# New orders, PSUM banks and DMA queues for a cross-attention and maxout-FFN kernel

## The chip, the cores and the metric

The kernel runs on one core of a Trainium2 chip. The metric is the device time of one execution in microseconds (us). A core has a matrix engine (PE, with its weight loads shown as PEld), a vector engine (DVE), a scalar engine (ACT), a third elementwise engine (POOL), and SP, which here only starts DMA transfers. ACT and POOL start DMA transfers too, each in its own queue; POOL's transfers also cast float32 to bfloat16 on the way. Matmul results go to PSUM, from where DVE or ACT must copy them before the bank can be used again.

## The reference

```python
scores = scale * x @ state.T            # x: (8, 8, 512, 64), state: (8, 8, 32, 64), scale 1/8
a = softmax(scores);   xread = a @ state
a2 = softmax(scale * state @ x.T);  sread = a2 @ x
t = concat([xread, sread], axis=2)      # 8 batches of 544 tokens, 8 heads of 64
t = t.transpose(0, 2, 1, 3).reshape(4352, 512)
h = maximum(maximum(t @ w1, t @ w2), t @ w3)     # 512 -> 768
out = h @ w_out                                  # 768 -> 512
```

The softmaxes subtract a row's maximum in the reference; the kernel leaves this out on its normal path and looks at the sums at the end (`look`, `flag`, `vl`), to go through a second, safe path only if they have left a range.

## The kernel before

The work of one batch is a chain. x is loaded with a cast to bfloat16 (`lxg` a half with every second head, `lx` the whole; `lxu` loads without a cast and `cxu` casts). It is turned so that the head dimension lies on the partitions: for batches 0 and 1 by PE (`xt`, line 233) with a copy from PSUM (`xtc`), for the others by a transposing DMA on SP's queue (`xtd`, line 245). Scores (`sc`, line 258) go through exp on ACT (`ex`, line 265); DVE sums and takes the reciprocal (`sum`, lines 272 and 274); the weights are the product of both (`wt`, line 280, on POOL or DVE as the plan says). They are turned by PE (`at`, copy `atc`) or by a transposing DMA on SP (`atd`, line 298). The states' read of x is `sr` (line 323), scaled by DVE (`srs`), turned by DMA on SP (`srt`, line 342) and placed (`ap`, line 347). For `sr` of batches 2 on, POOL makes a padded copy of x (`pad`, line 307).

State and W are multiplied first: G = state times W (`g` for a slice of 128 columns of w1, w2 and w3, `gr` for a run of columns, line 359; copies `gc`, `grc` on ACT, DVE, or half each, "AD"). Layer 1 of a batch is then six blocks `l1 b m` (line 412), each three accumulations of 512 columns in three PSUM banks: aT times G. The first goes through ACT (`m0`, line 427), DVE takes the maximum with the second (`ma`, line 432) and the third (`mb`, line 436). Layer 2 (`l2`, line 443) multiplies with w_out four times per batch, each with a copy to the output tile (`l2c`, line 450) and stores for two at a time (`so`, line 473). The states' tokens of all batches go through the same layers at the end as a batch "s" of 256 tokens (`l1s`, `l2 s`, `l2p s`); the end also splits layer 2 of batch 7 into parts of 128 or 256 columns (`l2p`, line 458, copy `l2pc`, store `sop`). W is loaded on POOL's queue by `lw m0 m1 i`: columns 128 m0 to 128 m1 of matrix i; w_out by `lwo` (line 182), states by `lst` (line 150). `busy n` issues n matmuls of zeros into a bank that nobody reads (line 207).

All of this is ordered by hand. Three texts of operations, FIRST, EACH and LAST, are performed in order; every engine takes its instructions in that order and waits only for data and buffers. A letter at the end of an operation is the engine or queue: D DVE, A ACT, P POOL, S SP.

```python
    perform(FIRST)
    for b in range(2, B - 1):
        perform(EACH, b)
    perform(LAST)
```

FIRST holds batches 0 and 1 and the beginning of 2. In EACH the batch number is added to an operation's first number: with -1 layer 2 of the batch before, with 0 layer 1, with 1 scores and G of the next, with 2 and 3 turning and loading x further ahead; an operation for a batch beyond 7 is left out.

PSUM has eight banks: four single ones (b0 to b3) and two pairs (w0, w1). BANKS and PAIRS give, one digit per tile in the order of the text, which one is taken; a tile waits until the copy of the last tile in its bank is done.

```python
    def bank(shape, dtype, name):
        return pp.tile(shape, dtype, tag="b" + next(homes["b"]), bufs=1, name=name)
```

The first steps on POOL's queue are the three cast loads of x (batch 1's first half, batch 0's second, batch 1's second), then W in pieces of 128 to 512 columns.

Of the kernel before, what the change touches and what calls it, by code (L numbers as in the profile page):

```python
# [45 lines left out]
LAST = """
    srt 7; srt 5; l1 7 0; l2 6 3; l1 7 2; ap 5 A; l2 6 1; srt 6; l1 7 3; m0 7 0; ma 7 0; mb 7 0; ap 6 A;
    ap 7 D; m0 7 2; l2c 6 3 D; l2c 6 1 A; l1 7 4; m0 7 3; l1s 0; m0 7 4; ma 7 2; mb 7 2; ma 7 3; mb 7 3;
    l1 7 1; l2 6 0; m0 s 0; ma 7 4; m0 7 1; l2c 6 0 A; ma s 0; mb 7 4; ma 7 1; mb s 0; mb 7 1; l1 7 5;
    m0 7 5; l1s 2; ma 7 5; mb 7 5; m0 s 2; l2p 7 1 384 512; l1s 1; ma s 2; l2p 7 0 384 512; l2p 7 3 256 512;  # L50
    l2pc 7 1 384 512 A; l2 6 2; m0 s 1; sop 7 1 384 512 S; l2p 7 3 0 256; ma s 1; l2p 7 2 128 384;
    l2pc 7 0 384 512 D; l1s 5; l2pc 7 3 256 512 A; l2c 6 2 A; l2p 7 0 0 128; mb s 2; l1s 3; l1s 4; mb s 1;
    l2pc 7 2 128 384 D; m0 s 5; l2p 7 2 0 128; l2p 7 2 384 512; l2p 7 0 128 256; l2pc 7 3 0 256 A;
    l2p 7 1 0 128; m0 s 3; look; ma s 5; sop 7 3 256 512 S; l2pc 7 0 0 128 D; sop 7 2 128 384 S; m0 s 4;
    sop 7 0 384 512 S; mb s 5; sop 7 0 0 128 A; ma s 3; so 6 2 3 P; so 6 1 2 S; so 6 3 4 S; so 6 0 1 P;
    l2pc 7 2 0 128 A; ma s 4; mb s 3; l2p 7 0 256 384; mb s 4; l2pc 7 0 128 256 D; flag; l2p s 0 0 256;
    l2pc 7 2 384 512 A; sop 7 0 128 256 S; sop 7 2 384 512 S; l2pc 7 1 0 128 A; l2pc 7 0 256 384 D;
    l2pc s 0 0 256 D; sop 7 2 0 128 S; l2p 7 1 128 384; l2 s 1; l2p s 0 256 512; sop 7 1 0 128 A;
    l2pc 7 1 128 384 A; sop 7 3 0 256 S; sop 7 0 256 384 S; sop s 0 0 256 S; vl; l2c s 1 D; sop 7 1 128 384 A;
    sos 1 A; l2pc s 0 256 512 D; sop s 0 256 512 A;  # L60
"""
# [606 lines left out]
```

## Time and profile before

| what | value |
|---|---|
| three timed runs | 155.39, 155.70, 155.71 us; median 155.7 |
| the profiled execution | 155.16 us, of which the profile's span is 153.3 |
| busy: PE, DVE, ACT, POOL | 146.6, 108.8, 88.9, 52.0 us |
| layer 1 (288 matmuls of 512 columns), layer 2 (168) | 66.7 and 40.6 us busy |
| fillers (26) | 8.4 us busy, 1.3 to 13.8 us |
| first layer-1 matmul | 16.69 us |
| one round of EACH | 15.25 us |

A timeline row has the start, the length, the engine, the source line, output and inputs with shapes, the number of instructions merged, and in brackets the idle time before with what ended it. PE's rows overlap by design: matmuls are pipelined, so six of 512 columns start within 1.29 us although each is 0.38 us long. The chain of work is followed back from the last instruction; its rows have start, length and work. In the DMA view a row gives the issuing queue, the number of transfers, the size and the median time from issue to landing.

### The profile page before, as it was taken

The numbers are of one execution on the slowest core, as the hardware profiler recorded it, in microseconds if no ns is written. First come the engines' busy times: TensorE is split into PE (matmuls) and PEld (weight loads), VectorE is DVE, ScalarE is ACT, GpSimd is POOL, SyncE is SP. The second block draws the span as 40 slices with busy tenths as digits, with TensorE's granted clock in tenths as the row PEclk, the third lists the DMA queues.
The fourth block names the chain that finished last, engine by engine and source line by source line (L and its number), as shares of the span: only waits on it lengthen the run. The fifth ranks groups of instructions, "written<-read, shape, count | busy, mean of one in ns | idle before, by whom it ended". The sixth has DMA issues, their size and how long they took to land.

```text
span 153.3 us, 3610 instructions
## 1 busy us (share of the span) xinstructions
PE 146.6 (96%) x1429; PEld 73.8 (48%) x1429; DVE 108.8 (71%) x191; ACT 88.9 (58%) x148; POOL 52.0 (34%) x69
## 2 busy tenths in 40 slices
PE   6989999999999999999999999999999999999970
PEld 2566433453454444444444444444344445679940
DVE  3568788799967696778677867786778757645540
ACT  0676887865576577647764776477647644324300
POOL 6999509411229105610571064106410100002000
PEclk9999999999999999999999999999999999999998
DMA  4999999999969997998499930823070300005563
GB/s 117 236 193 203 194 190 194 162 185 195 197 179 166 258 213 220 140 186 166 147 132 194 176 136 3 176 45 137 4 214 17 137 2 4 0 17 193 188 189 114
DMA packets 39477, 22.30 MB, mean 145 GB/s; under 512 B 23584, under 2 KB 37408, under 8 KB 39456
## 3 DMA queue, kind: packets, MB, share of 16 engines
q0 software_dynamic: 14944, 10.75, 40.9%
q1 hardware_dynamic: 22640, 7.21, 27.0%
q10 hardware_dynamic: 1872, 4.06, 7.7%
q8 instruction: 12, 0.20, 0.6%
q14 instruction: 9, 0.07, 0.2%
HBM read 15.20 MB, written 8.91 MB: 157 GB/s over the span
## 4 chain that ended last, share of the span: by engine, by line
PE 88%; DMA 4%; issue 1%; DVE 1%; POOL 1%; ACT 1%; POOLq 0%
PE pw L412 45%; PE po L443 25%; PE pg L359 6%; DMA x<-in_x_dram 4%; PE po L458 4%; PE psr L323 2%; PE ps L258 2%; PE idle L207 1%; POOL x L166 1%; PE pat L291 1%; PE pgh L359 1%; PE pt L218 1%; ACT t L427 0%; DVE xT L240 0%; DVE osb L450 0%
## 5 line engine op out<-in xcount | busy, mean ns | idle before, releaser
L412 PE MATMUL pw<-aT,G 128*128 128x512 bf16 x288 | 66.7, 379 | 0.0
L432 DVE TENSOR_TENSOR t<-t,pw 128x512 bf16<-128x512 bf16 (+1 forms) x54 | 35.1, 650 | 14.7 <-ACT t L427 11.9
L427 ACT CAST t<-pw 128x512 bf16<-128x512 f32 (+1 forms) x54 | 30.8, 569 | 21.9 <-PE pw L412 19.9
L412 PEld LDWEIGHTS <-G 128*128 128x128 bf16 x288 | 27.1, 98 | 33.3 <-issue 1.8
L443 PE MATMUL po<-wout,ht 128*128 128x512 bf16 x168 | 40.6, 379 | 0.1
L436 DVE TENSOR_TENSOR ht<-t,pw 128x512 bf16<-128x512 bf16 x48 | 32.9, 687 | 4.4
L473 POOL DMA_DIRECT2D out_dram<-osb x8 | 4.8, 600 | 66.5 <-ACT osb L450 43.9
L443 PEld LDWEIGHTS <-ht 128*128 128x128 bf16 x168 | 15.3, 97 | 19.6 <-issue 2.7
L450 ACT COPY osb<-po 128x512 f32<-128x512 f32 x24 | 13.6, 590 | 10.9 <-PE po L443 10.9
L399 ACT CAST G<-pg 128x1024 bf16<-128x1024 f32 x18 | 17.7, 1019 | 3.1 <-PE pg L359 3.1
L280 POOL TENSOR_TENSOR a<-e,rden 128x1024 bf16<-128x1024 bf16 (+1 forms) x9 | 14.6, 1640 | 12.9 <-DVE rden L274 6.5
L272 DVE TENSOR_REDUCE seen<-e 128x32 f32<-128x1024 bf16 (+1 forms) x10 | 9.9, 993 | 6.8 <-ACT e L265 6.8
L307 POOL COPY xp<-x 128x1024 bf16<-128x1024 bf16 x12 | 12.3, 1062 | 5.1 <-DMA x<-in_x_dram 5.1
L359 PE MATMUL pg<-w,bd 64*32 64x512 bf16 (+1 forms) x288 | 11.8, 364 | 0.0
L265 ACT ACTIVATE e<-ps 128x1024 bf16<-128x1024 f32 (+1 forms) x10 | 8.5, 854 | 4.1 <-PE ps L258 2.9
L377 ACT CAST G<-pg 128x768 bf16<-128x768 f32 x11 | 8.9, 808 | 2.8 <-PE pg L359 2.8
L207 PE MATMUL idle<-zero 128*128 128x512 bf16 x26 | 8.4, 470 | 1.3 <-DVE zero L185 1.3
L412 PE MATMUL pw<-atp,w 128*128 128x256 bf16 x72 | 8.7, 273 | 0.0
L177 POOL DMA_DIRECT2D w<-in_moe_w_dram x10 | 7.6, 776 | 0.0
L412 PEld LDWEIGHTS <-w 128*128 128x128 bf16 x72 | 7.0, 98 | 1.2
L359 PEld LDWEIGHTS <-bd 64*32 64x32 bf16 x336 | 3.5, 89 | 8.0 <-issue 7.2
L399 DVE CAST G<-pg 128x1024 bf16<-128x1024 f32 x6 | 7.3, 1209 | 0.0
(66 smaller groups left out, 106.5 us busy)
## 6 DMA issues: line engine op xcount, KB each, us to landing
out_dram<-osb ACTq DMA_DIRECT2D x6, 512.0 KB, 4.4
out_dram<-osb POOLq DMA_DIRECT2D x6, 512.0 KB, 3.1
x<-in_x_dram POOLq DMA_DIRECT2D x4, 512.0 KB, 8.3
x<-in_x_dram POOLq DMA_DIRECT2D x7, 256.0 KB, 6.3
w<-in_moe_w_dram POOLq DMA_DIRECT2D x3, 256.0 KB, 8.2
wout<-in_moe_w_out_dram POOLq DMA_DIRECT2D x1, 768.0 KB, 10.0
w<-in_moe_w_dram POOLq DMA_DIRECT2D x5, 128.0 KB, 8.2
osb<-in_x_dram SPq DMA_DIRECT2D x1, 512.0 KB, 4.1
```

The lines of the kernel that those rows point to most:

```text
L207: nc.tensor.matmul(p, zero[:, 0:128], zero, start=True, stop=True)
L272: nc.vector.reduce_sum(out=den, in_=parity(e[b], g), axis=AX.X)
L280: times[c](out=parity(a[b], g).rearrange("p j g s n -> p j (g s) n"), in0=parity(e[b], g).rearrange("p j g s n -> p j (g s) n"), in1=rdens ...
L307: nc.gpsimd.tensor_copy(out=xp[b][:, :, :, g * (D + 1):g * (D + 1) + D], in_=v[:, g])
L359: nc.tensor.matmul(p(s, g), bd(b, 2 * s + g)[64 * g:64 * g + 64, g, :], f(w_sb[64 * g:64 * g + 64, s]), start=True, stop=True, tile_positi ...
L399: copier[c[g]](out=v[:, g:h], in_=p[:, g:h, 0:c1 - c0])
L412: nc.tensor.matmul(pw[i][:, 0:n], lhs(i, k), rhs(k), start=(k == 0), stop=(k == nk - 1))
L427: nc.scalar.copy(out=t0s[b, m][:, 0:n], in_=open_ps["l", b, m][0][:, 0:n])
L432: nc.vector.tensor_max(t1s[b, m][:, 0:n], t0s.pop((b, m))[:, 0:n], open_ps["l", b, m][1][:, 0:n])
L436: nc.vector.tensor_max(ht[b][:, m, :], t1s.pop((b, m))[:, 0:n], open_ps.pop(("l", b, m))[2][:, 0:n])
L443: nc.tensor.matmul(p, ht[b][:, m, j * 128:(j + 1) * 128], wout_sb[:, m, :], start=(m == 0), stop=(m == NM - 1))
L450: copier[c[i]](out=o[:, j, i * w:i * w + w], in_=p[:, i * w:i * w + w])
```

## The change

All plans are written anew; the functions that perform them are the same. In FIRST the fillers are spread in ones and twos, the ACT table is loaded by an early `warm`, W comes in other pieces (columns 0 to 256 of w1 and w3 and 0 to 128 of w2 first; the last pieces are three of 384 columns), `lwo` and half of batch 3's x are issued before `pad 2` and so ahead of batch 2's turning, and some copies change engine (`wt 1 1` to POOL, `wt 2` to DVE, `gc 0 0` to `gc 0 2` to DVE). In EACH, layer 2 of two rows comes before the G runs and scores behind the first block of layer 1; the load of x moves from the round's start to its end, behind a store; the store of rows 0 and 1 moves from ACT's queue to SP's, ahead of `xtd`; `xtd` and `srt` both stand ahead of `atd`. LAST ends on other parts of layer 2, and stores are spread anew over the three queues.

```diff
--- before.py
+++ after.py
@@ -16,57 +16,59 @@
 
 
 FIRST = """
-    zero; busy 10; clr 3; lxu 0 0 S; lxg 1 0; lst 0 A; lxg 0 1; clr 1; busy 1; stc 0 D; clr 0; ident;
-    lxg 1 1; busy 2; lw 0 2 1; stt 0; lst 1 S; cxu 0 0 D; xones 0; xt 0 0; stp 0 A; busy 2; xt 1 0;
-    xtc 0 0 D; sc 0 0; busy 4; warm; xtc 1 0 D; lw 0 1 2; xt 0 1; sc 1 0; lw 0 4 0; xt 1 1; ex 0 0;
-    xtc 0 1 A; sc 0 1; xones 1; sum 0 0; stc 1 P; ex 1 0; lw 1 3 2; xtc 1 1 D; lw 3 5 2; ex 0 1; lw 2 3 1;
-    sum 1 0; sc 1 1; stt 1; busy 6; lw 3 6 1; lxg 2 1; wt 0 0 P; ex 1 1; at 0 0; sum 0 1; sr 0; atc 0 0 A;
-    clr 2; busy 1; wt 1 0 P; stp 1 A; wt 0 1 P; at 1 0; sum 1 1; at 0 1; wt 1 1 D; g 0 0; lxg 2 0; sr 1;
-    atc 0 1 A; srs 1; at 1 1; g 1 0; g 1 1; gc 0 0 A; atc 1 0 D; l1 0 0; atc 1 1 A; ones; g 0 1; gc 1 0 A;
-    gc 1 1 D; m0 0 0; gc 0 1 A; xtd 2; l1 1 0; g 0 2; srs 0; m0 1 0; lw 5 6 0; g 1 2; l1 1 1; ma 0 0;
-    lw 5 6 2; lw 4 5 0; l1 0 1; pad 2; mb 0 0; g 1 3; gc 0 2 A; m0 1 1; gc 1 2 A; ma 1 0; lxg 3 1; g 0 3;
-    l1 0 2; m0 0 1; gc 0 3 A; m0 0 2; l1 1 2; g 0 4; mb 1 0; g 0 5; ma 1 1; l1 0 3; gc 1 3 A; lst 2 A; lwo;
-    mb 1 1; l1 1 3; m0 1 2; ma 0 1; g 1 4; gc 0 4 A; g 1 5; m0 0 3; gc 0 5 A; l1 0 5; mb 0 1; ma 0 2;
-    m0 1 3; mb 0 2; gc 1 4 A; m0 0 5; l1 1 4; ma 1 2; mb 1 2; ma 0 3; ma 1 3; l1 0 4; mb 0 3; mb 1 3;
-    ma 0 5; mb 0 5; m0 1 4; m0 0 4; gc 1 5 A; sc 2 -; lxg 3 0; ma 1 4; mb 1 4; gr 2 1024 1280; lst 3 S;
-    gr 2 0 512; ex 2 -; xtd 3; l1 1 5; ma 0 4; gr 2 512 1024; grc 2 1024 1280 D; lx 4; gr 2 1792 2304;
-    mb 0 4; stc 3 P; sum 2 -; grc 2 0 512 A; grc 2 1792 2304 D; stc 2 P; l2 0 2; m0 1 5; l2 0 3;
-    gr 2 1280 1792; l2c 0 2 D; wt 2 - P; stt 2; grc 2 1280 1792 A; l2 0 1; grc 2 512 1024 A; ma 1 5; mb 1 5;
-    l2 0 0; stp 2 D; stt 3; sr 2; stp 3 A; l2c 0 3 D; so 0 2 4 A; l2c 0 1 D; l2c 0 0 A; srs 2; so 0 0 2 P;
-    atd 2;
+    lxg 1 0; lst 0 A; zero; clr 2; lxg 0 1; busy 1; lst 1 A; busy 2; clr 0; busy 1; busy 1; ident;
+    stc 0 D; lxu 0 0 S; busy 1; busy 1; lxg 1 1; xones 0; lw 0 2 0; clr 3; stt 0; warm; ones; busy 1;
+    busy 1; busy 1; stp 0 DA; busy 1; cxu 0 0 D; busy 1; clr 1; busy 1; lw 0 2 2; xt 0 0; xt 1 0;
+    xtc 1 0 A; busy 2; xtc 0 0 D; busy 1; sc 0 0; lw 0 1 1; xt 0 1; sc 1 0; busy 1; xtc 0 1 D; busy 1;
+    ex 0 0; stc 1 P; sum 0 0; busy 1; ex 1 0; xt 1 1; sc 0 1; xones 1; xtc 1 1 D; busy 1; busy 1; stt 1;
+    lw 1 3 1; lw 2 3 2; busy 1; sc 1 1; lw 2 3 0; wt 0 0 P; lw 3 6 2; busy 1; busy 1; busy 1; ex 0 1;
+    sum 0 1; at 0 0; ex 1 1; lw 3 6 1; busy 1; sum 1 0; sum 1 1; stp 1 A; wt 0 1 P; sr 0; g 0 0; g 1 0;
+    gc 0 0 D; atc 0 0 A; wt 1 0 P; sr 1; at 0 1; srs 0; srs 1; g 0 1; gc 1 0 A; atc 0 1 A; g 1 1;
+    wt 1 1 P; l1 0 0; lw 3 6 0; lxg 2 0; gc 0 1 D; m0 0 0; at 1 0; ma 0 0; gc 1 1 A; at 1 1; g 0 2;
+    lxg 2 1; mb 0 0; g 1 2; gc 0 2 D; atc 1 0 A; atc 1 1 A; l1 0 1; l1 0 2; l1 1 0; m0 0 1; ma 0 1;
+    xtd 2; lst 2 S; l1 1 1; g 0 3; m0 0 2; m0 1 0; mb 0 1; ma 0 2; gc 1 2 A; lwo; m0 1 1; mb 0 2;
+    ma 1 0; ma 1 1; mb 1 0; lxg 3 1; g 1 3; l1 1 2; gc 0 3 AD; gc 1 3 A; g 0 5; m0 1 2; g 1 4; pad 2;
+    l1 0 3; gc 0 5 A; l1 1 3; m0 0 3; gc 1 4 A; mb 1 1; ma 1 2; g 0 4; mb 1 2; m0 1 3; ma 0 3; lxg 3 0;
+    g 1 5; gc 0 4 A; l1 0 5; l1 1 4; stc 2 P; m0 0 5; mb 0 3; gc 1 5 A; ma 1 3; mb 1 3; l1 0 4; ma 0 5;
+    m0 1 4; l1 1 5; m0 0 4; gr 2 512 1024; mb 0 5; m0 1 5; xtd 3; gr 2 1024 1280; ma 1 4; mb 1 4;
+    gr 2 1280 1792; ma 0 4; mb 0 4; ma 1 5; grc 2 1280 1792 A; l2 0 1; sc 2 -; lst 3 A; l2 0 0; l2 0 2;
+    grc 2 1024 1280 AD; ex 2 -; grc 2 512 1024 A; mb 1 5; l2c 0 0 A; stt 2; gr 2 1792 2304; sum 2 -;
+    wt 2 - D; l2c 0 1 D; gr 2 0 512; l2c 0 2 A; sr 2; grc 2 1792 2304 D; stc 3 P; l2 0 3; l2c 0 3 D;
+    so 0 2 4 P; stp 2 A; stt 3; grc 2 0 512 AD; lx 4; so 0 0 2 P; stp 3 A; atd 2; srs 2;
 """
 EACH = """
-    gr 1 1792 2304; lx 3; gr 1 0 512; l2 -1 3; sc 1 -; grc 1 0 512 A; pad 1; l2 -1 0; ex 1 -; l1 0 0;
-    l2 -1 1; grc 1 1792 2304 D; gr 1 1280 1792; gr 1 1024 1280; srt -2; xtd 2; sum 1 -; l2c -1 3 A;
-    gr 1 512 1024; sr 1; l2c -1 0 A; m0 0 0; l1 0 1; ma 0 0; l1 0 2; l2c -1 1 A; so -1 0 2 A; mb 0 0;
-    grc 1 1024 1280 DA; l1 0 3; srs 1; m0 0 1; m0 0 2; ma 0 1; m0 0 3; mb 0 1; wt 1 - P; l1 0 5; m0 0 5;
-    l2 -1 2; grc 1 1280 1792 A; grc 1 512 1024 A; ma 0 2; l1 0 4; mb 0 2; ma 0 3; mb 0 3; ma 0 5; m0 0 4;
-    mb 0 5; ma 0 4; mb 0 4; l2c -1 2 A; atd 1; ap -2 A; so -1 2 4 P;
+    pad 1; l2 -1 0; l2 -1 1; gr 1 1792 2304; gr 1 1024 1280; l2c -1 1 D; l2c -1 0 A; grc 1 1792 2304 AD;
+    gr 1 0 512; l1 0 0; sc 1 -; grc 1 1024 1280 A; so -1 0 2 S; l2 -1 3; m0 0 0; xtd 2; l1 0 1; ex 1 -;
+    gr 1 1280 1792; grc 1 0 512 DA; ma 0 0; mb 0 0; sum 1 -; srt -2; gr 1 512 1024; l2c -1 3 A; m0 0 1;
+    sr 1; l1 0 2; grc 1 1280 1792 A; l1 0 3; ma 0 1; m0 0 2; l1 0 5; wt 1 - P; mb 0 1; srs 1; l1 0 4;
+    ma 0 2; mb 0 2; m0 0 3; m0 0 5; m0 0 4; ma 0 3; mb 0 3; grc 1 512 1024 A; l2 -1 2; ma 0 5; atd 1;
+    l2c -1 2 A; so -1 2 4 P; ma 0 4; mb 0 4; lx 3; mb 0 5; ap -2 A;
 """
 LAST = """
-    srt 7; srt 5; l1 7 0; l2 6 3; l1 7 2; ap 5 A; l2 6 1; srt 6; l1 7 3; m0 7 0; ma 7 0; mb 7 0; ap 6 A;
-    ap 7 D; m0 7 2; l2c 6 3 D; l2c 6 1 A; l1 7 4; m0 7 3; l1s 0; m0 7 4; ma 7 2; mb 7 2; ma 7 3; mb 7 3;
...
-    l2pc 7 2 0 128 A; ma s 4; mb s 3; l2p 7 0 256 384; mb s 4; l2pc 7 0 128 256 D; flag; l2p s 0 0 256;
-    l2pc 7 2 384 512 A; sop 7 0 128 256 S; sop 7 2 384 512 S; l2pc 7 1 0 128 A; l2pc 7 0 256 384 D;
-    l2pc s 0 0 256 D; sop 7 2 0 128 S; l2p 7 1 128 384; l2 s 1; l2p s 0 256 512; sop 7 1 0 128 A;
-    l2pc 7 1 128 384 A; sop 7 3 0 256 S; sop 7 0 256 384 S; sop s 0 0 256 S; vl; l2c s 1 D; sop 7 1 128 384 A;
-    sos 1 A; l2pc s 0 256 512 D; sop s 0 256 512 A;
+    l1 7 0; l2 6 1; m0 7 0; ma 7 0; l2c 6 1 A; mb 7 0; l1 7 2; m0 7 2; srt 7; l1 7 3; m0 7 3; ma 7 2;
+    ma 7 3; l2 6 3; srt 5; ap 5 A; ap 7 A; srt 6; mb 7 2; mb 7 3; l1 7 4; ap 6 A; l2c 6 3 A; m0 7 4;
...
+    l2pc 7 2 384 512 D; sop 7 0 0 128 S; l2p 7 0 128 256; l2p s 0 0 256; l2pc 7 3 0 256 D;
+    l2pc 7 2 0 128 A; l2pc 7 2 128 384 D; l2c s 1 D; l2pc 7 3 256 512 A; l2pc 7 1 128 384 A;
+    l2pc 7 0 128 256 A; flag; sop 7 3 0 256 A; sop 7 2 384 512 A; l2pc s 0 0 256 D; sop 7 0 128 256 A;
+    sop 7 2 0 128 S; sop 7 1 128 384 S; l2 6 2; sop s 0 0 256 A; sop 7 2 128 384 S; sop 7 0 384 512 P;
+    l2p s 0 256 512; l2pc s 0 256 512 D; l2c 6 2 A; l2p 7 1 0 128; so 6 2 3 A; l2pc 7 1 0 128 D;
+    sop 7 0 256 384 S; sos 1 S; sop s 0 256 512 A; sop 7 1 384 512 P; sop 7 1 0 128 A;
+    sop 7 3 256 512 P; vl;
 """
 
 BANKS = """
...
 """
 PAIRS = """
-    0101010110 1010100010 1010010100 1010010100 10
+    0101010110 1010001010 0101001010 0101001010 01
 """
```

More of the change, by code (lines that the diff above doesn't have):

```diff
@@ L45 @@
+    ma 0 2; mb 0 2; m0 0 3; m0 0 5; m0 0 4; ma 0 3; mb 0 3; grc 1 512 1024 A; l2 -1 2; ma 0 5; atd 1;
+    l2c -1 2 A; so -1 2 4 P; ma 0 4; mb 0 4; lx 3; mb 0 5; ap -2 A;
 """
 LAST = """
-    srt 7; srt 5; l1 7 0; l2 6 3; l1 7 2; ap 5 A; l2 6 1; srt 6; l1 7 3; m0 7 0; ma 7 0; mb 7 0; ap 6 A;
-    ap 7 D; m0 7 2; l2c 6 3 D; l2c 6 1 A; l1 7 4; m0 7 3; l1s 0; m0 7 4; ma 7 2; mb 7 2; ma 7 3; mb 7 3;
-    l1 7 1; l2 6 0; m0 s 0; ma 7 4; m0 7 1; l2c 6 0 A; ma s 0; mb 7 4; ma 7 1; mb s 0; mb 7 1; l1 7 5;
@@ L50 @@
[L50 to L54, printed above, removed]
@@ L55 @@
-    sop 7 0 384 512 S; mb s 5; sop 7 0 0 128 A; ma s 3; so 6 2 3 P; so 6 1 2 S; so 6 3 4 S; so 6 0 1 P;
-    l2pc 7 2 0 128 A; ma s 4; mb s 3; l2p 7 0 256 384; mb s 4; l2pc 7 0 128 256 D; flag; l2p s 0 0 256;
-    l2pc 7 2 384 512 A; sop 7 0 128 256 S; sop 7 2 384 512 S; l2pc 7 1 0 128 A; l2pc 7 0 256 384 D;
-    l2pc s 0 0 256 D; sop 7 2 0 128 S; l2p 7 1 128 384; l2 s 1; l2p s 0 256 512; sop 7 1 0 128 A;
-    l2pc 7 1 128 384 A; sop 7 3 0 256 S; sop 7 0 256 384 S; sop s 0 0 256 S; vl; l2c s 1 D; sop 7 1 128 384 A;
@@ L60 @@
-    sos 1 A; l2pc s 0 256 512 D; sop s 0 256 512 A;
+    l1 7 0; l2 6 1; m0 7 0; ma 7 0; l2c 6 1 A; mb 7 0; l1 7 2; m0 7 2; srt 7; l1 7 3; m0 7 3; ma 7 2;
+    ma 7 3; l2 6 3; srt 5; ap 5 A; ap 7 A; srt 6; mb 7 2; mb 7 3; l1 7 4; ap 6 A; l2c 6 3 A; m0 7 4;
+    l1s 0; so 6 3 4 S; l1 7 1; m0 s 0; l2 6 0; ma 7 4; m0 7 1; l1 7 5; l1s 2; l1s 1; mb 7 4; l2c 6 0 A;
+    ma s 0; mb s 0; m0 7 5; so 6 1 2 S; l1s 5; l1s 3; ma 7 1; mb 7 1; ma 7 5; m0 s 2; mb 7 5; m0 s 1;
+    m0 s 5; l1s 4; ma s 2; ma s 1; l2p 7 1 384 512; mb s 2; m0 s 3; l2p 7 0 0 128; ma s 5; m0 s 4;
@@ new lines @@
+    l2p 7 2 0 128; l2p 7 0 384 512; l2p 7 0 256 384; mb s 1; l2p 7 2 128 384; l2p 7 3 256 512;
+    l2p 7 2 384 512; l2p 7 3 0 256; so 6 0 1 S; ma s 3; mb s 3; mb s 5; l2pc 7 1 384 512 A; ma s 4;
+    mb s 4; l2pc 7 0 0 128 D; l2pc 7 0 256 384 D; l2p 7 1 128 384; l2 s 1; l2pc 7 0 384 512 D; look;
+    l2pc 7 2 384 512 D; sop 7 0 0 128 S; l2p 7 0 128 256; l2p s 0 0 256; l2pc 7 3 0 256 D;
+    l2pc 7 2 0 128 A; l2pc 7 2 128 384 D; l2c s 1 D; l2pc 7 3 256 512 A; l2pc 7 1 128 384 A;
+    l2pc 7 0 128 256 A; flag; sop 7 3 0 256 A; sop 7 2 384 512 A; l2pc s 0 0 256 D; sop 7 0 128 256 A;
@@ L66 @@
-    3123013203 1201321032 0132013021 0230213021 0320323102 3021320130 120312013
[3 rows of a table added]
 """
 PAIRS = """
-    0101010110 1010100010 1010010100 1010010100 10
+    0101010110 1010001010 0101001010 0101001010 01
 """
```

2 lines of the change are left out of this document (removed), and 3 rows, old and new, of the table BANKS.

## The prediction

> **What bounds the kernel now.** I read the page's busy times first, then the chain in time order, then the timelines of PE, DVE, POOL and SP from 0 to 50 us and of the last 10 us, then the DMA landings, asked for issue by issue.
>
> ```profile
> PE 146.6 (96%) x1429; PEld 73.8 (48%) x1429; DVE 108.8 (71%) x191; ACT 88.9 (58%) x148; POOL 52.0 (34%) x69
> ...
> PE   6989999999999999999999999999999999999970
> ```
>
> PE is busy for 146.6 of 153.3 us. The changed orders issue the same instructions, PE's above all (26 fillers in both); only the split of G casts, the engine of some copies and the queues differ. So PE's sum is fixed, and time can come only from the two ends, or from new gaps between.
>
> ```profile
> 3.56 6.19 DMA x<-in_x_dram
> 9.75 0.05 issue
> 9.80 0.64 PE pxt L233 x8
> 10.43 0.02 issue
> 10.46 0.70 DVE xT L240
> 11.16 0.05 issue
> 11.21 0.41 PE ps L258 x8
> 11.61 0.22 PE pt L218 x4
> 11.84 1.29 PE idle L207 x6
> ```
>
> Until 9.75 us PE waits for the last piece of batch 1's x; nothing before it can gain. After it six fillers still stand (and a seventh at 13.85). The first layer-1 matmul comes at 16.69. From there to 148.55 PE has no gap that I can see: the range of interest is 9.8 to 16.7 us and the tail.
>
> ```profile
> 147.73 0.82 PE L458 MATMUL po<-wout,hts 128*128 128x256 bf16 x6
> 147.93 0.69 DVE L450 COPY osb<-po 128x512 f32<-128x512 f32 x1 [1.52 <-PE po L443]
> 148.58 0.42 DVE L462 COPY osb<-po 128x256 f32<-128x256 f32 x1
> 148.65 1.15 ACTq L481 DMA_DIRECT2D out_dram<-osb  x1
> 149.90 0.55 ACTq L466 DMA_DIRECT2D out_dram<-osb  x1
> ```
>
> PE ends at 148.55. The last store is ready at 149.0, but stands behind a store that holds ACT's queue for 1.15 us, and goes out at 149.90; it lands 2.4 us later, at 152.3, 3.75 after PE's end.
>
> **Part 1, the start.** x's three pieces keep their places at the head of POOL's queue, so 9.75 stays. Then, by PE's new order (8 transposes 0.45, scores 0.23, filler 0.216, 4 transposes 0.22, sr 0.56, one G slice 0.30): xt 1 1 ends at 10.25, sc 0 1 10.48, two fillers, stt 1 and a filler 11.35, sc 1 1 (its xT copy, on DVE behind a sum, is ready at 11.2) 11.56, three fillers 12.2, at 0 0 (its weights leave POOL at about 11.55: sum at 10.5 plus 3.11/3) 12.42, a filler that waits for its bank until ex 1 1 has ended at 12.6, sr 0 13.38, two G slices 14.0, sr 1 14.56, at 0 1 14.8. The next G slices wait for the copies of the first two: on DVE the new gc 0 0 runs 14.05 to 15.0 (0.96, the row of the one DVE G cast, behind four sums), on ACT gc 1 0 ends at 15.1. They end at 15.65; l1 0 0 waits for aT on ACT, 15.6, and starts at **15.7** instead of 16.69. Behind it now stand at 1 0 and at 1 1 (0.44), ahead of it g 0 1 (0.29): **gain 0.99 - 0.15 = 0.84**.
>
> W's pieces. By landings POOL's queue carried 896 KB between x's end at 9.76 and the 512-column piece's landing at 14.3, and 1,024 KB more to 19.9: 190 KB per us. m = 0 now needs 640 KB instead of 896: 13.1 us by the first rate, wanted at 13.4. All of m = 1 and 2 follow 512 KB later, 15.7, wanted at 17.4; the last piece, with 2,304 KB, at 22, wanted by g 0 3 at 23.4. It is issued behind four weights on POOL (1.04 each, one of them DVE's before), at 16.2, while the queue still has data until 19.9: costs nothing. Cover gone: each us late is a us of PE.
>
> x of batch 2 then lands at 24.8 (before 22.6), w_out at about 33 to 34.5 (768 KB at 175 KB per us beside a transposing transfer that took 6.0 us and a queue that moved 640 KB in 8.4 us beside it), wanted at 35.3. Batch 3's last half at 36 to 37; its transposing transfer and then aT 2 stand in order on SP: aT 2 issues at 41.4 (sc 2 at 36.8, ex 2, sum, weights on DVE: 512 columns took 0.69, so 1.0 to 1.4), lands after 3.0 to 4.4 at 44.4 to 45.8; l1 2 0 wants it at 46.2. Nothing, slack 0.4.
>
> **Part 2, layer 1 of batches 0 and 1.** DVE takes gc 0 0, 0 1, 0 2 and half of 0 3, and gives up gc 1 1, an aT copy (0.41) and weights (0.69). A block of layer 1 is 1.30 on PE and 1.39 on DVE (rows 18.11, 18.89, and the next at 19.5 if nothing waits). From 15.7: 12 blocks, 0.44, and 8 slices at 0.225 are 17.8 us of PE; on DVE 16.7 plus 2.4 of casts plus 0.9 for sr are 20.0, over PE's 17.8, and only four single banks stand between. DVE's lead of work may trail PE by 1.5 us, as after the first block (18.09 to 19.58), so I walked the banks: small waits at g 1 2, l1 0 2, l1 1 2, l1 1 3 and l2 0 1, 0.1 to 0.3 each, with gaps in what the change removes elsewhere. **Cost 0.25**, between 0 and 0.7 (2.2 - 1.5).
>
> **Part 3, the loop (five rounds of 15.25).** The same PE work. Two places become tight: ex, now behind l1 0 0 and scores at 4.7 of the round, gives the sum at 6.4, its reciprocal, ma and mb of the next block, and sr's scaling at 9.9, whose bank l1 2's successor wants at 10.0; mb 0 1 frees a bank at 9.45 for 9.55. **Cost 0.2 in all**, between 0 and 1.0 (0.2 a round). Splitting casts over DVE and ACT adds 0.2 to DVE's 11 to 12 us a round: hidden under PE. The store of rows 0 and 1 goes from ACT's queue (0.34) to SP's: it saves no time on ACT that matters.
>
> SP is the dangerous queue. x for two batches on is loaded at the round's end, behind a store that waits for the last layer-2 copy: 1.4 us into the next round. Then in order on SP: the transposing transfer that waits for that x (2.6), srt (1.4), then aT, wanted at 18.65.
>
> ```profile
> x<-in_x_dram POOLq DMA_DIRECT2D x1, 512.0 KB, 9.7
> ...
> x<-in_x_dram POOLq DMA_DIRECT2D x1, 512.0 KB, 6.7
> ...
> x<-in_x_dram POOLq DMA_DIRECT2D x1, 512.0 KB, 7.0
> ```
>
> These are the loads issued at 45.63, 59.68 and 75.16. With L for the landing and 4.4 for aT's, aT is there at 1.4 + L + 2.6 + 1.4 + 4.4 = 9.8 + L: in time while L is under 8.85 (10.2 with aT's best, 3.0). With one store ahead L was 6.7 and 7.0; a second store now starts 2 us after the load, at most 1.3 more: 8.0 to 8.3. Nothing, and the rival below if not.
>
> **Part 4, the tail.** Last are now a state part of 256 columns and 128 columns of batch 7; the state's 512-column store (1.15) leaves earlier, on SP. With E as PE's end: l2c 6 2 on ACT ends at E - 0.25, its store issues to E + 0.2, the state part (copied at E + 0.2) to 0.8, the last (0.29 copy) to 1.15, landing 2.4 from its start: E + 3.2 instead of 3.75. **Gain 0.5**, between 0 (3.5 us was seen for a part in a crowd) and 1.
>
> **Sum**: - 0.84 + 0.25 + 0.2 - 0.5 = - 0.9. The profiled execution took 155.16 (span 153.3, 1.9 around it), so 154.3; the three timed runs have a median of 155.7, 0.54 more, so on that scale **154.8**. Differences under 0.2%, 0.31 us, can't be told from none here.
>
> **The clock.** The fillers' weight loads stand 0.43 us apart from 1.68 to 5.09 us, and then three in 0.60: PE went from half to full pace after 3.9 us of unbroken fillers. Now seven fillers run, then four transposes of states (from 4.3), then six. [...]
>
> **Rivals.**
> 1. *The start gains, the banks take it back.* Parts 2 and 3 at their upper ends: - 0.84 + 0.7 + 1.0 - 0.5 = + 0.35, at the middle - 0.3: 155.4 to 156.0, say 155.6. For it: DVE's 20.0 against 17.8. Against: DVE idles in the loop for 3 us a round. Chance 0.18.
> 2. *Slower: aT waits on SP for the x load.* Each us of L over 8.85 is a us in each of four rounds. Even is L = 8.85 + 0.9/4 = 9.1; at the 9.7 once seen it costs 3.4, giving 155.7 - 0.9 + 3.4 = **158.2**. For it: the first round has three stores beside the load, as 45.63 had two and a transposing transfer; against: the two others at 6.7 and 7.0. If only the first round waits, 0.85 goes and the time is 155.65. Chance 0.17.
> 3. *The pace changes late.* If PE stays at half pace for a further 3.9 us from 5.2, half of that is lost, less the 0.4 of waiting before 9.8: + 1.5, giving 156.3. For it: fillers broken by transposes; against: no gap over 0.05 us. Chance 0.07.
> 4. *The forecast*, 0.58, own range 154.0 to 155.3; low end with Part 4 at 1 and Parts 2 and 3 at nothing: 153.9.
>
> The range is 153.9 to 157.2: it leaves out the last third of rival 2 and what lies under 153.9. Faster 0.60 (the forecast, a little of rival 1), same 0.15, slower 0.25.
>
> **What would show it.** Right: the first pw matmul at 15.5 to 15.9; no PE gap over 0.3 before E; last store landing 3.2 after E. Wrong: PE waits for W's DMA before 14 or near 23; DVE named before pw between 17 and 34; PE waiting for aT near each round's first pw, with SP's aT transfer issued over 14 us into the round; the fillers' loads 0.43 apart beyond 5.5.

## The result, and the profile after

The changed kernel takes 158.2 us, median of five runs (157.30 to 163.08), beside 155.48 for the kernel before: ratio 1.0161, 95% interval 1.0137 to 1.0185. The forecast was 154.8. The same kernel was run in two more sets: 156.2 us both times, ratios 1.0042 (1.0017 to 1.0068) and 1.0042 (1.0008 to 1.0076), with single runs from 154.88 to 162.82. So it is slower than before, by 1.6% in one set and 0.4% in two, and its time depends on something that differs between executions. The ratios in this document leave out runs more than 1.5% above the fastest of their kernel; one of these is the 163.08 us run, the profiled one of the first set, whose profile shows the loss enlarged.

Line numbers are 2 higher here than in the kernel before. First the page: busy time, PE's slices, the granted clock.

```profile
PE 148.3 (92%) x1429; PEld 74.6 (46%) x1429; DVE 110.8 (69%) x196; ACT 88.5 (55%) x155; POOL 52.4 (32%) x70
...
PE   6999999997999993299999999999999999999970
...
PEclk9999999999999999569999999999999999999998
```

The instructions are the same 1429, but PE has a dent in slice 10 (36 us) and a hole in slices 16 and 17 (60 to 68 us). The granted clock falls to 0.50 within the hole, at 64.5 us, and is full again from 71.3. PE's timeline names dent and hole:

```profile
37.22 0.64 PE L260 MATMUL ps<-bd,xT 128*128 128x64 bf16 x16 [0.86 <-DMA xT<-x]
...
61.68 0.40 PE L361 MATMUL pg<-w,bd 64*32 64x512 bf16 x8
67.38 2.74 PE L414 MATMUL pw<-aT,G 128*128 128x512 bf16 x6 [5.29 <-DMA aT<-a]
```

Scores of batch 2 wait 0.86 us for xT, and layer 1 of batch 3 waits 5.29 us for aT. Its first six matmuls then take 2.74 us instead of the 1.47 of later rounds, at half clock. SP's timeline, and the DMA view of the stretch (queue, size, us from issue to landing):

```profile
25.16 5.45 SPq L247 DMA_TRANSPOSE xT<-x  x1
...
55.59 3.11 SPq L247 DMA_TRANSPOSE xT<-x  x1
58.75 1.22 SPq L344 DMA_TRANSPOSE ats<-sr  x1
60.08 1.42 SPq L300 DMA_TRANSPOSE aT<-a  x1
```

```profile
x<-in_x_dram POOLq DMA_DIRECT2D x4, 256.0 KB, 8.3
wout<-in_moe_w_out_dram POOLq DMA_DIRECT2D x1, 768.0 KB, 10.5
xT<-x SPq DMA_TRANSPOSE x1, 12.0
```

The transposing transfer of batch 2's x takes 12.0 us beside w_out and batch 3's x. In the profile before the change, where those loads were issued behind it, it took 6.0:

```profile
xT<-x SPq DMA_TRANSPOSE x1, 6.0
```

Twenty us later x of batch 4 is loaded, issued at 45.43, where it was 26.97 before:

```profile
x<-in_x_dram POOLq DMA_DIRECT2D x1, 512.0 KB, 10.1
```

The transposing transfer that waits for this x goes out at 55.59, and aT, behind it and srt, at 60.08. (xtd and srt stood ahead of atd before the change too, but there the x had come long before; what is new is the late load.) The load of batch 5's x is issued at 60.35, and the two travel side by side:

```profile
x<-in_x_dram POOLq DMA_DIRECT2D x1, 512.0 KB, 9.9
aT<-a SPq DMA_TRANSPOSE x1, 7.3
```

The start is as forecast: PE goes on when x has come, with small gaps, and the first layer-1 matmul is at 15.47 (forecast 15.7, before 16.69). PE's timeline:

```profile
9.97 0.61 PE L235 MATMUL pxt<-ident,x 128*128 128x128 bf16 x8
...
15.02 0.52 PE L361 MATMUL pg<-w,bd 64*32 64x384 bf16 x16
15.47 1.10 PE L414 MATMUL pw<-aT,G 128*128 128x512 bf16 x4
```

The end, ACT's queue (PE ends at 156.16, the last store lands at 160.18):

```profile
156.07 0.35 ACTq L475 DMA_DIRECT2D out_dram<-osb  x1
156.51 1.60 ACTq L468 DMA_DIRECT2D out_dram<-osb  x1
158.21 0.55 ACTq L470 DMA_DIRECT2D out_dram<-osb  x1
```

A store of 128 KB (the state part of 256 columns) holds the queue for 1.60 us with the last one behind it: the landing is 4.0 us after PE's end, not 3.2 (3.7 before).

### The profile page after: what moved, and what is told of

Same layout as the page of the kernel before. It is cut to its first block, busy times and chain, and to the rows that moved or that the text cites. A ratio compares the mean times of both kernels' runs of the same rounds, so it can differ in the third digit from the quotient of the medians.

```text
span 161.3 us, 3620 instructions
## 1 busy us (share of the span) xinstructions
PE 148.3 (92%) x1429; PEld 74.6 (46%) x1429; DVE 110.8 (69%) x196; ACT 88.5 (55%) x155; POOL 52.4 (32%) x70
## 4 chain that ended last, share of the span: by engine, by line
PE 55%; DMA 4%; DVE 0%; issue 0%
PE pw L414 31%; PE po L445 15%; DMA aT<-a 4%; PE po L460 4%; PE pg L361 2%; PE ps L260 1%; PE psr L325 1%; DVE osb L464 0%; PE pgh L361 0%; PE pst L502 0%
## 5 line engine op out<-in xcount | busy, mean ns | idle before, releaser
L414 PE MATMUL pw<-aT,G 128*128 128x512 bf16 x288 | 68.4, 385 | 5.5 <-DMA aT<-a 5.5
L445 PE MATMUL po<-wout,ht 128*128 128x512 bf16 x168 | 39.5, 381 | 0.1
L401 ACT CAST G<-pg 128x1024 bf16<-128x1024 f32 (+1 forms) x23 | 18.6, 807 | 7.7 <-PE pg L361 7.7
L282 POOL TENSOR_TENSOR a<-e,rden 128x1024 bf16<-128x1024 bf16 (+1 forms) x9 | 13.6, 1528 | 24.9 <-ACT t L429 21.9
L452 ACT COPY osb<-po 128x512 f32<-128x512 f32 x21 | 12.5, 595 | 10.2 <-PE po L445 8.0
L475 POOL DMA_DIRECT2D out_dram<-osb x7 | 4.2, 593 | 37.5 <-ACT osb L452 31.8
L309 POOL COPY xp<-x 128x1024 bf16<-128x1024 bf16 x12 | 12.4, 1071 | 3.5 <-DMA x<-in_x_dram 3.5
L452 DVE COPY osb<-po 128x512 f32<-128x512 f32 x8 | 5.5, 689 | 10.2 <-PE po L445 10.2
L209 PE MATMUL idle<-zero 128*128 128x512 bf16 x26 | 9.3, 488 | 1.3 <-DVE zero L187 1.3
L401 DVE CAST G<-pg 128x512 bf16<-128x512 f32 (+1 forms) x12 | 8.3, 730 | 1.6 <-ACT G L401 1.6
L470 POOL DMA_DIRECT2D out_dram<-osb x3 | 1.6, 541 | 20.6 <-DVE osb L464 20.5
L379 ACT CAST G<-pg 128x768 bf16<-128x768 f32 (+1 forms) x9 | 6.8, 770 | 1.4 <-PE pg L361 1.4
## 6 DMA issues: line engine op xcount, KB each, us to landing
wout<-in_moe_w_out_dram POOLq DMA_DIRECT2D x1, 768.0 KB, 10.5
```

The costliest lines, as they stand in the source:

```text
L209: nc.tensor.matmul(p, zero[:, 0:128], zero, start=True, stop=True)
L282: times[c](out=parity(a[b], g).rearrange("p j g s n -> p j (g s) n"), in0=parity(e[b], g).rearrange("p j g s n -> p j (g s) n"), in1=rdens ...
L309: nc.gpsimd.tensor_copy(out=xp[b][:, :, :, g * (D + 1):g * (D + 1) + D], in_=v[:, g])
L401: copier[c[g]](out=v[:, g:h], in_=p[:, g:h, 0:c1 - c0])
L414: nc.tensor.matmul(pw[i][:, 0:n], lhs(i, k), rhs(k), start=(k == 0), stop=(k == nk - 1))
L445: nc.tensor.matmul(p, ht[b][:, m, j * 128:(j + 1) * 128], wout_sb[:, m, :], start=(m == 0), stop=(m == NM - 1))
```

## The experiments

Each set ran with the kernel before on the same chip (155.45 to 155.60 in all five). Edits are to the changed kernel, named "after", unless said.

**Which text carries the loss.** One of the three texts with its bank digits is new, the other two are as before; and after once more.

```diff
 first_new: FIRST new, EACH and LAST as before
 each_new:  EACH new, FIRST and LAST as before
 last_new:  LAST new, FIRST and EACH as before
```

> The changed kernel once more, for a second profile and more timed runs. Its first profile shows PE waiting 5.3 us for batch 3's transposed weights (aT) at 62 to 67 us, and the clock at half for some us behind the wait. Theory A (x of batch 4 is loaded too late, so that its transposing transfer and then aT stand late on SP's queue): about 158, a wait for aT in round 1 of the loop, and none in the later rounds. Rival (the later rounds or layer 1's banks take the time): 158 with waits spread over all rounds.

> Only FIRST and its banks are new; loop and end are the old ones. Theory A: the late load of batch 4's x stands in FIRST, so most of the loss comes with it: the start gains 1.2, the wait for batch 2's turned x costs 0.9, the wait for aT 2.5 or more: 157.5 to 158.5. Rival B (the new loop's order on SP's queue and its tight banks lose the time): 155.2 to 155.6, since the start's gain and the wait for turned x about cancel.

> Only the loop EACH and its banks are new. Theory A: batch 4's x is loaded early again by the old FIRST, the later loads land some 8 us after their issue and so in time: 155.2 to 155.8, no wait for aT over 0.3 us. Rival B: 157 to 158, with a wait for aT in every round or many small waits for DVE and ACT.

> Only LAST and its banks are new. By the profile of the changed kernel the last store landed 4.0 us after PE's end, against 3.75 before: theory A says 155.6 to 156.0 (0.1 to 0.4 more). The prediction on record had 0.5 less: 155.0.

Measured: after_again 156.2, 1.0042; first_new 160.04 (157.33 to 164.01), 1.0161 (1.0112 to 1.0210); each_new 157.55, 1.0120 (1.0095 to 1.0144); last_new 156.25, 1.0046 (1.0026 to 1.0067). The mixtures have waits of their own at the joints, where bank digits of two texts meet: 1.48 us in each_new, ending at 45.13, and 0.89 in last_new, ending at 120.76, both absent from after. That is why neither kept its forecast. Between its two joints each_new shows no wait for aT and none for a bank, so rival B (the loop's order on SP and its tight banks) falls; some 0.5 us of its loss has no wait to its name. first_new, with the old loop, has DMA waits:

```profile
PE pw L411 <- DMA aT<-a: 3.4, 1, 3.4
PE ps L257 <- DMA xT<-x: 2.1, 2, 1.7
PE pg L358 <- DVE G L398: 1.3, 2, 0.8
...
PE pg L358 <- DMA w<-in_moe_w_dram: 0.6, 1, 0.6
PE pxt L232 <- DMA x<-in_x_dram: 0.5, 1, 0.5
```

(PE's waits: us in total, times, longest.) They are mostly not after's. The old loop begins with its own load of x, so the loads of batches 4 and 5 follow each other at 45.63 and 47.06, which neither kernel does; the wait for aT and 1.74 of the 2.1 us for xT (that of batch 4) come behind them, and only 0.34 is the wait for xT of batch 2. So this mixture says little of after. The surprise is after_again: its profile has the wait for xT, 1.1 us, and none for aT. Theory A, a load of x that is always too late, holds only in some executions.

**xT of batch 2.**

```diff
 x3_behind   (FIRST)  -... mb 1 0; lxg 3 1; g 1 3; ... pad 2;   +... mb 1 0; g 1 3; ... pad 2; lxg 3 1;
 wout_behind (FIRST)  -... gc 1 2 A; lwo; ... pad 2;            +... gc 1 2 A; ... pad 2; lwo;
```

> The changed kernel with the first half of batch 3's x (lxg 3 1) issued behind pad of batch 2 instead of ahead of it, as before the change; w_out stays ahead. Theory C (the transposing transfer of batch 2's x, 12.0 us where it took 6.0, is slow because of the loads that stand in POOL's queue beside it): half of the bytes that the change put ahead move away, so xT of batch 2 lands after 8 to 11 us, at 34 to 36.5 instead of 37.4, and the wait of scores of batch 2 for it (0.9 to 1.1 us) shrinks to 0 to 0.5: 0.5 to 1.0 us faster than the changed kernel, 155.2 to 155.7. Rival: POOL's queue still carries 1.25 MB beside the transfer in any order, the transfer takes as long as the loads do, 12 us, and the time stays 156.2; then w_out itself is the cause.

> The changed kernel with w_out, not batch 3's half, moved behind pad of batch 2 on POOL's queue, and nothing else. Theory C (the transposing transfer of batch 2's x is as slow as the loads beside it are many): xT of batch 2 lands after 6.5 to 9.5 us instead of 10.5 to 12.4, and scores of batch 2 do not wait. But w_out, issued at 27.5 instead of 19, lands at 36 to 38, and layer 2 wants it at 35.3: PE waits 0.7 to 2.7 us for wout instead. Time 155.8 to 158. Rival: without its 768 KB in the way the queue has w_out landed by 35.3 all the same; then 154.9.

Measured: x3_behind 154.88 (154.52 to 156.67), 0.9977 (0.9950 to 1.0004): 1.3 us less than after by the medians, 1.0 by the two ratios, from two sets. wout_behind 159.02 (155.86 to 162.89, six runs). The transposing transfer took 12.0, 11.8 and 10.5 us in three profiles of after, 9.7 with 256 KB moved behind it, 8.0 with 768 KB moved, 6.0 before the change with both behind. Over all profiles it is 10.5 to 12.4 with both ahead (eight), 8.5 to 10.3 with 256 KB behind (eight), 8.0 with 768 KB behind (one), and 4.5 to 8.0 with the old order (three). x3_behind:

```profile
wout<-in_moe_w_out_dram POOLq DMA_DIRECT2D x1, 768.0 KB, 10.9
...
xT<-x SPq DMA_TRANSPOSE x1, 9.7
```

In x3_behind PE waits for no DMA from the first layer-1 matmul to its end, at 147.70 (before: 148.55). In wout_behind scores do not wait, but layer 2 does (and x came late at the start of this execution):

```profile
PE po L443 <- DMA wout<-in_moe_w_out_dram: 3.9, 1, 3.9
PE pxt L233 <- DMA x<-in_x_dram: 1.6, 1, 1.6
```

Theory C holds. The wait does not come in each execution: after_third's profiled run (154.88) has a transfer of 10.5 us, and no wait for xT. w_out has to stand ahead of batch 2's turning in this order of PE; batch 3's x must not. The rows go this far: the transfer was slower with each load beside it, 12.0 us in after against 9.7 in x3_behind and 6.0 before, and on average by more the more bytes there were. How the queues share the DMA engines they do not show.

**aT of batch 3.**

```diff
 x_early   (FIRST) lx 4 behind "stc 2 P" instead of behind "grc 2 0 512 AD"; (EACH) lx 3 first instead of near the end
 x_late    (FIRST) -lx 4; so 0 0 2 P;   +so 0 0 2 P; lx 4;
 at_ahead  (EACH)  -m0 0 0; xtd 2; l1 0 1; ... atd 1;   +m0 0 0; l1 0 1; ... atd 1; xtd 2;
```

> The changed kernel with x loaded a round earlier again: x of batch 4 is issued on POOL behind the first of the two casts of states (near 38 us instead of 45.8), and each round's load of x stands at the round's start, as before the change. Theory A (the load of x is too late, so that the transposing transfer of batch 4's x and then aT of batch 3 stand late on SP): xtd of batch 4 goes out at about 47.5 instead of 54.5 to 55.6, aT of batch 3 at its earliest near 57.5, and PE waits nothing for it in any execution, so the spread of the runs shrinks and the median falls by what the wait cost in the middle, 0.3 to 1.5 us against the changed kernel (156.2 on the last chip): 154.8 to 156.0. Price of the move: aT of batch 2, in flight at 42 to 46, now stands beside x of batch 4 and may land up to 1 us later. Rival B (chance collisions of the transfers in the round, whoever is first): the wait for aT 3 comes as often as before and the time stays at 156.2 or above.

> The changed kernel itself once more, beside the next three. It has been 158.2 us in one set and 156.2 in another. Theory D (a cliff): aT of batch 3 wants to be landed at 62.1; issued at 58.7 it lands 2.7 us later, in time; issued at 60.1, as in the profile with the 5.3 us wait, it travels together with the load of batch 5's x (issued at 60.4) and takes 7.3. So the time has two values, near 155.5 to 156.5 without the wait and 158 to 163 with it, and how often the wait comes decides the median of a set. Rival E: the time of a set moves as a whole with the chip, 0.5% up or down, and this set is again either all near 156.2 or all near 158.2 without a wait for aT in its profile.

> The changed kernel with one move in the loop: xtd (x of two batches on) stands behind atd on SP's queue, not ahead of it, so aT waits for no load of x. Theory D: aT of batch 3 goes out when its weights are ready, near 53.7 instead of 58.7 to 60.1, and lands long before 62; no execution waits for it, so the runs above 157.5 vanish, and the median falls by 0 to 0.7 us on a set like the one with 156.2, to 155.6 to 156.2, and by 2 us on a set like the one with 158.2. The other 1 us, the wait of scores of batch 2 for xT, stays. Rival F (the move only hands the wait on): the transposing transfer of batch 4's x now leaves behind aT at 55, or, where it waits for its x, at 55.6, and scores of batch 4 wait for it at 64; then nothing is gained.

> The changed kernel with the load of batch 4's x moved behind the last store of the joint (so 0 0 2 on POOL), 0.6 us later than now, and nothing else. Theory D: this puts aT of batch 3 at 59.3 instead of 58.7 where all goes well, over the edge more often; the share of runs with the wait rises and the median goes up by far more than 0.6 us, to 157 to 159. Rival: without a cliff, 0.6 us less slack of the 0.7 seen costs nothing, and at most 0.6: 156.2 to 156.8.

Measured, with all runs in order:

| kernel | median | ratio, interval | runs |
|---|---|---|---|
| after_third | 156.24 | 1.0042 (1.0008 to 1.0076) | 154.88 to 156.47 (7), 157.06 to 158.00 (4), 162.82 |
| at_ahead | 155.80 | 1.0012 (0.9990 to 1.0034) | 155.24 to 156.24 (11), 158.34 |
| x_late | 157.77 | 1.0136 (1.0099 to 1.0173) | 156.77 to 157.82 (5), 162.61, 163.33, 165.46 |
| x_early | 157.34 | 1.0141 (1.0099 to 1.0184) | 156.97 to 158.84 (6) |

x_late moves one load behind a store, by some 0.6 us, and costs 1.5 in the median. Theory D's edge is there, though not in the terms it was forecast in: in x_late's profile aT goes out at 58.62, no later than in two profiles without a wait (58.69, 58.85). What is shorter is the distance to the next load. How far aT's issue lies ahead of the issue of batch 5's x, and how long aT then takes: 2.06 us ahead, 2.9 (after_third); 1.83, 2.8 (tail_sp, below); 1.78, 2.7 (after_again); 0.93, 4.3 (x_late); 0.27, 7.3 (after). PE wants it at about 61 to 62. The three runs of x_late from 162.61 up have no profile. x_late's row of PE and its DMA rows:

```profile
62.95 1.47 PE L412 MATMUL pw<-aT,G 128*128 128x512 bf16 x6 [1.67 <-DMA aT<-a]
```

```profile
x<-in_x_dram POOLq DMA_DIRECT2D x1, 512.0 KB, 9.3
...
aT<-a SPq DMA_TRANSPOSE x1, 4.3
```

at_ahead takes aT out of that race; SP issues it at 53.61:

```profile
53.61 1.25 SPq L298 DMA_TRANSPOSE aT<-a  x1
54.96 3.06 SPq L245 DMA_TRANSPOSE xT<-x  x1
```

11 of 12 runs lie within 1 us; what is behind the one at 158.34 no profile shows. The intervals of at_ahead and after_third overlap, so the gain is shown by the wait that is gone and by the spread, less by the median. Rival E falls, as after_third alone has runs of both kinds, and rival F: scores of batch 4 do not wait. x_early, my first cure, was a miss: aT of batch 3 no longer waits, but x of batch 4 now lies beside aT of batch 2, which takes 5.7 us and makes PE wait 1.3, more than the price I had set (1). How a set gets its share of waiting executions stays open; the first set had 157.3 or more in each run, and only its 163.08 us run has a profile.

**The tail.**

```diff
 tail_sp  -sop s 0 256 512 A;   +sop s 0 256 512 S;
 x3_tail  as x3_behind, and: sop s 0 0 256, sop s 0 256 512, sop 7 1 0 128 from A to S
 big_last as x3_at (below), so 6 2 3 A behind sop 7 1 0 128 A
 big_pool as x3_at, so 6 2 3 on P, last of POOL's queue
 fill_4, fill_10  as x3_at, -vl;  +busy 4; vl;  or  +busy 10; vl;
```

> The changed kernel with one letter changed: the store of the state part of 256 columns (the last but one on ACT's queue, issued there in 1.60 and 1.66 us) goes to SP's queue, which is empty from 147.1 on. Theory: the tail of the changed kernel, last landing 4.0 to 4.1 us after PE's end, is long because that issue holds ACT's queue while the last part's store stands behind it; without it the last store is issued at about 0.4 us after PE's end and lands 2 us later, near PE's end + 2.8 with the state part's store landing about then too: 1.1 to 1.3 us faster than the changed kernel, 155.0 against 156.2. Rival: the end is set by the landings themselves (seven stores in the last 5 us); then SP's issue or its landing takes as long as ACT's did and under 0.4 us goes.

> The changed kernel with half of batch 3's x behind pad of batch 2 (154.88 us alone) and three stores of the end moved from ACT's queue to SP's: both parts of the state's second row block and the last part of batch 7. In every profile so far the store that follows the 256 KB store on ACT's queue is held for 1.36 to 1.94 us, whichever it is. Theory G: ACT's queue is held by its own earlier stores (five in 2.8 us); on SP's queue, with two or three stores in the last 5 us, the last two go out at 0.2 to 1.0 us after PE's end, and the last landing comes 2.7 to 3.2 after PE's end instead of 3.8 to 4.1: 0.7 to 1.1 us off, 153.8 to 154.2. Rival: the hold is in the DMA engines (all 16 are full with the stores) and SP's stores are held as well: 154.9.

> As x3_at, with the 256 KB store of batch 6's rows (so 6 2 3) moved behind the two small stores on ACT's queue. In seven profiles one store of the end was held for 1.36 to 1.94 us, on ACT's queue or on SP's, and each time the hold ended within 0.2 us of the landing of the 256 KB store issued just before. Theory H: a store issued while that big one is in flight is held until it lands; then here the two small ones go out unheld at 0.2 and 0.7 us after PE's end, the big one at 1.2, and the last landing comes at 3.0 to 3.4 after PE's end instead of 3.8 to 4.1: 0.5 to 0.9 us faster than x3_at. Rival G (a queue holds whatever comes after so many stores): the hold falls on the second small store or the big one, and the last landing is at 4.2 to 4.8.

> As x3_at, with the 256 KB store on POOL's queue, behind all of POOL's other stores. [...]

> As x3_at (154.8 us), with four filler matmuls of 0.22 us (zeros into a bank that nobody reads) added on PE behind its last useful matmul, and nothing else. Theory I: the hold of a store comes from a fetch of instructions. In seven profiles the packet of 16 KB on the instruction queue starts within 0.13 us of PE's end with the new end (0.72 before it with the old one), and the held store is let go 0.36 to 0.40 us after that packet has come, at any place in any queue. If PE's end sets the fetch, 0.86 us of fillers put it off until the last store (at 0.75 after the last useful matmul) has been started: no store over 0.7 us long, last landing 2.9 to 3.3 us after the last useful matmul instead of 3.7 to 4.2, and 0.4 to 1.0 us less in all, 153.8 to 154.4, although PE does more. Rival G (the sixth store of a queue, or ACT's own traffic): the hold stays at 0.36 us with 1.4 to 1.8 us, time 154.8.

> As fill_4 with ten fillers, 2.16 us. Theory I: the fetch starts 2.1 us after the last useful matmul, the stores go out unheld as in fill_4, but the fetch itself (1.4 to 1.9 us, to 3.9) and what follows it at the end now come last: 0.3 to 1.0 us slower than fill_4, 154.3 to 155.2. Rival G: hold as before; 154.8 to 155.5.

Measured: tail_sp 156.31, 1.0045 (1.0022 to 1.0068), no gain; x3_tail 156.47, 1.0064 (1.0037 to 1.0092), 1.6 us worse than x3_behind; big_last 155.31, 0.9982 (0.9956 to 1.0007); big_pool 157.57, 1.0137 (1.0112 to 1.0162); fill_4 154.93, 0.9958 (0.9941 to 0.9974); fill_10 155.60, 1.0014 (0.9992 to 1.0035). All my cures failed, and the theories behind them fell. With the store taken off ACT's queue (tail_sp) the next one is held instead. On SP's queue (x3_tail) a store is held for 1.92 us, with three more behind it. With the 256 KB store last (big_last), a small store that follows a small one is held. With ten fillers two stores are held:

```profile
147.41 0.35 ACTq L473 DMA_DIRECT2D out_dram<-osb  x1
147.85 1.12 ACTq L466 DMA_DIRECT2D out_dram<-osb  x1
149.07 1.42 ACTq L468 DMA_DIRECT2D out_dram<-osb  x1
```

One thing is common to the 19 profiles that have such a hold, of 20. A packet of 16 KB on q8, which the profile calls an instruction queue, starts from 1.2 us before PE's end to just after it, moves when fillers move that end, and is done 0.35 to 0.42 us before the last held store is let go (0.16 in x3_behind). In after it lies from 156.17 to 157.72 and the store is let go at 158.11; before the change from 147.83 to 149.41, and 149.80: 0.39 us both times. The 20th, first_new, has the packet (done at 158.18) and no held store: the two issued at 157.54 and 158.28 take 0.65 and 0.55 us. In x3_at the stretch from 148.4 to 150.4 has it (q8), with three smaller ones (q14):

```profile
q10 hardware_dynamic: 260, 0.35, 49.0%
q14 instruction: 3, 0.02, 9.6%
q8 instruction: 1, 0.02, 5.6%
```

So where there is a hold, its end goes with that packet. That the packet, theory I's "fetch of instructions", causes it is argued, not shown: the theory forecast that fill_4 would be rid of the hold, and it had one of 1.84 us, a packet on q14 starting 0.3 us after the last useful matmul, as in x3_at. What is shown is that neither the queue, nor the size, nor PE's end sets it alone: four fillers behind PE's last useful matmul cost nothing (154.93 against 154.80). In big_pool the program ended 4.1 us after its last landing, 1.0 to 1.5 in the other profiles.

**Both waits undone.** all_three is x_early, tail_sp and x3_behind together; x3_at is x3_behind and at_ahead together.

> The three edits together: x a round earlier, the state part's store on SP, half of batch 3's x behind pad of batch 2. If each theory holds: no PE wait for aT of batch 3, 0 to 0.5 us for xT of batch 2, last landing under 3 us after PE's end: 153.6 to 154.4, under the kernel before (155.56 on the last chip) by 1.1 to 2.0 us. If the two DMA theories fall and only the tail holds, 155.0.

> The changed kernel with the two DMA edits that helped: half of batch 3's x behind pad of batch 2 (154.88 us alone), and xtd behind atd on SP's queue in the loop (155.8 alone). If the two waits, of scores of batch 2 for xT (0.9 to 1.5 us in most profiles) and of layer 1 of batch 3 for aT (0 to 5.3, by chance), are all that the change lost, this kernel has no PE wait for a DMA, PE's end near 147.7, no run above 156, and a median of 154.5 to 154.8, which is what was forecast for the change. If a third loss exists, the median stays above 154.9 or the spread stays.

Measured: all_three 155.10 (154.14 to 160.85), 0.9967 (0.9938 to 0.9995); with x_early in it, it keeps a wait for aT of batch 2, 0.7 us. x3_at 154.80 (154.09 to 155.68), 0.9956 (0.9936 to 0.9977). It is 0.4% faster than the kernel before and keeps all else of the change; its ten runs lie in 1.6 us. It can't be told from x3_behind (154.88), whose profile has no wait for aT either (issued 1.66 us ahead of the next load, landed after 2.8): what at_ahead adds on top of x3_behind is not shown. This is x3_at's list of PE's waits behind the start:

```profile
PE pg L359 <- DMA w<-in_moe_w_dram: 0.3, 1, 0.3
```

## Why the prediction was wrong

The step that failed is the last paragraph of Part 1, "Nothing, slack 0.4", with the paragraph on SP in Part 3, "Nothing, and the rival below if not". They price two orders at nothing: w_out and half of batch 3's x issued ahead of batch 2's turning, and x loaded at the round's end, ahead of an xtd that holds up aT. What the runs showed in place of nothing is a wait of 0.3 to 1.3 us for xT of batch 2 and one of 0 to 5.3 us for aT of batch 3. With half of batch 3's x back behind, and xtd moved behind atd, neither wait is left and the kernel takes 154.80. That this is the forecast time is partly luck, as the last paragraph of this section says.

- **Start, - 0.84**: right. The first layer-1 matmul comes at 15.3 to 16.0 in 16 of the 17 profiles with the new FIRST, against 16.69; the 17th, at 16.6, had its x 1.6 late.
- **W's pieces, nothing**: nearly. PE waited 0.2 to 0.9 us for W, between 23 and 25.4, in 6 of the 17; there the slack of 1.4 was gone.
- **xT of batch 2**: wrong. I took the 6.0 us of before to find w_out's rate, and never asked what w_out does to the transfer. It became 10.5 to 12.4, against a want at 36.4; PE waited 0.3 to 1.3 where the wait came, and aT 2, behind it, lands at 46.7 in after, not 44.4 to 45.8 (a wait of 0.23). x3_behind gives 1.0 to 1.3 for the whole.
- **Banks in Parts 2 and 3, + 0.45**: too much. x3_behind's PE end is 0.85 ahead of before, of which the start gives 1.07: 0.2 is left for both. Three more profiles in which PE waits for no DMA behind the first layer-1 matmul (x3_tail, big_pool, fill_10) give the same 0.2.
- **SP's queue**: the mechanism was rival 2's, in the first round alone, as its last sentence says ("If only the first round waits, 0.85 goes"). Its threshold for L, 8.85, sorts the eight profiles in which batch 4's x is loaded late and xtd stands ahead of atd: no wait for aT at L of 8.5 to 8.8, a wait at 9.4 (x_late) and 10.1 (after). The price was wrong in kind. 9.8 + L takes aT's landing as 4.4 and charges a us for a us. But a late aT meets the next load of x: 2.7 us becomes 7.3, and then, in the profiled run, the granted clock is 0.50 for 6.8 us. There L was 10.1 instead of 8.0 to 8.3, xtd and srt took 4.5 of SP instead of 4.0, and aT 7.3 instead of 4.4. Over six profiles L was 8.6 to 10.1. Rival 2's 158.2 is the first set's time by chance: it charged 0.85 in each of four rounds, and the later rounds do not wait (in the profiled run the second load takes 9.9, in a round in which PE is late itself, and the last two 8.2 and 7.8).
- **The clock's share**: in the profiled run PE works from 67.4 to 71.3 at half clock, which loses half of 3.9, 2.0. 5.29 + 0.23 + 0.86 + 2.0 = 8.4, and the run is 8.6 over x3_behind's profiled one (154.52).
- **Tail, - 0.5**: wrong in sign. Last landing 3.8 to 4.2 after PE's end instead of 3.7, so + 0.1 to + 0.5. I priced the last two stores with 0.6 and 0.35 of issue; the first of them takes 1.4 to 1.8.
- **Rivals 1 and 3**: no. In no profile of the changed kernel is DVE named before PE between 17 and 34 us, and full clock began at 6.5 us in the first profile of after (5.2 before), ahead of the last of x, for which PE goes on at 9.97.

Without the waits the terms add up, but not as forecast. x3_behind has - 0.85 at PE's end, where the forecast had - 0.84 + 0.25 + 0.2 = - 0.39, and + 0.1 in the tail, where it had - 0.5: two errors of some 0.5 us that cancel. 154.88 against 155.52, and 154.80 against 155.50, are gains of 0.6 and 0.7; the forecast gain was 0.9, counted from 155.7.

## What to carry to other kernels

Price a DMA that is moved by what it does to the transfers beside it, not only by its own landing; a transposing transfer on SP went from 4.5 to 8.0 us to 10.5 to 12.4 under loads that were moved ahead of it by a few us. Where a transfer waits for a load and another waits behind it in the queue, look for the next load that the late one will meet: past that edge the cost here was a cliff (aT took 2.7 to 2.9 us on one side, 4.3 and 7.3 on the other), and a single profile shows one side of it. Put the transfer that PE wants first ahead of the one that still waits.
